# Half of the rows of a late w_down tile: their last 768 columns in eleven small transfers into the ring

## The chip, the cores and the metric

One core of a Trainium2 chip runs the kernel. The metric is the device time of one execution in microseconds (us), as a median of several runs. The core has five engines, here named as in the profile: PE (matrix multiply; PEld is its loading of weights), DVE (vector), ACT (scalar), POOL (GpSimd) and SP (sync), which here issues nearly all DMA transfers. The transfers run on 16 DMA engines.

## What is computed

One step of a decoder layer for a single token, with two branches on the same normalised input, both added to `x`. All is float32.

```
xn = layernorm(x)                                  # 1024
q  = xn @ wq                                       # 32 heads of 128
o  = softmax(q k^T / sqrt(128)) v                  # 4 kv heads, last 4096 cache rows
A  = o @ wo                                        # 4096 x 1024
h  = gelu(xn @ w_gate) * (xn @ w_up)               # 3584
B  = h @ w_down                                    # 3584 x 1024
out = x + A + B
```

With one token, each weight is read once and used once.

## The kernel before

**Staging.** All weights and the two caches pass through one SBUF tile, `ring`, of 128 partitions by 32,768 floats. `PLAN` (L256 to L263) lists the loads in order: a key, its place in the ring, and the key whose use must be done before it. `used(key)` (L346) issues the loads that wait for `key`. The semaphores are worked out by `Flow` (L54): it records each instruction, finds which earlier ones it overlaps in memory, and on a second pass gives each DMA a semaphore of its own and each reader the waits it needs. All instructions go through L99 to L107, so the profile shows one line for nearly everything, L225.

**The end of the run.** `wo` comes as `o0` and `o1` (16 tiles each, a tile being 128 rows by 1024 columns). `w_down` has 28 tiles: `d0` has 16, `d1` 8, `d2` 4. `d1` and `d2` go where `o1` was, so they are issued as the tiles of `o1` are used up. `d2` is at column 24,576 of the ring; each partition holds 4 rows of `w_down`, one for each tile, 4,096 bytes apiece.

`outputs` (L724) and `downs` (L734) multiply. A tile is used in one of two ways. `accumulate` (L715) makes four PE matmuls into the PSUM tile `out_p`, one for each quarter of the columns. `add_scaled` (L417) makes one DVE instruction that adds the tile, scaled by a number per partition, into the SBUF tile `out_part`. In `downs`, DVE takes the six tiles in `KEPT`, all of `d0`; PE takes the rest, folds in `out_part`, and then takes the tiles of `d2`.

The last tile is treated apart (L749 to L768). After tile 2 of `d2` DVE makes `y = out_p + x_out`. PE multiplies columns 0 to 511 of the last tile into `first_p`, DVE adds it to the first half of `y`, and two stores are issued. PE multiplies columns 512 to 1023 into `last_p`, and DVE adds it in two pieces to `y_last`, each followed by a store.

**How `d2` is loaded (L319 to L330).** Tiles 0 and 1 of `d2` are taken as 2,048 columns of 128 partitions. Partitions 0, 2, 4... come whole in one transfer (64 x 2048), partitions 1, 5, 9... whole in one (32 x 2048). Partitions 3, 7, 11... come without their last 768 columns (32 x 1280); these columns of the ring are zeroed by a POOL memset (L321), so that the matmuls on them add nothing. Tile 2 comes in one transfer, and tile 3 in three: columns 0 to 511, 512 to 767 and 768 to 1023 (L328, where `end == rows` picks the last tile; `rows` is the number of tiles, 4).

The 32 x 768 values left out have a buffer of their own, `moved` (L332), loaded by ten small transfers of 3 or 5 rows (`load_moved`, L335), which `PLAN` puts between `o1` and `d0`. `hidden` (L664) gathers the matching values of `h` with four small matmuls and four DVE copies into `moved_h`, and `downs` adds the product with two `add_scaled` (L737, L738).

Of the kernel before, what the change touches and what calls it, by code (L numbers as in the profile page):

```python
# [5 lines left out]
F32 = mybir.dt.float32  # L6
# [5 lines left out]
P = 128  # L12
D = 1024
# [19 lines left out]

ROW = (31, 32, 95, 96)
MC = 768
MOVED = ((0, 0, 0, 12, 4), (0, 1, 12, 12, 4), (1, 0, 24, 5, 1), (1, 1, 29, 3, 1))
SIZES = {"tp": NB, "acc": 2 * NB, "part": 8 * NB, "rows": 2 * NB}


# [14 lines left out]
class Flow:  # L54
# [4 lines left out]
    def __init__(self, nc, plan=None):  # L59
        self.nc = nc  # L60
        self.plan = plan
        self.ops = []
        self.touched = {}
        self.sems = {}
        if self.plan:
            inc = self.plan[-1][1]
            self.last = inc
            used = {key for waits, _ in self.plan for key, _ in waits}
            used.update(inc for _, inc in self.plan if inc is not None)
            for key in [*sorted(used - {inc}), ISSUED, inc]:  # L70
                self.sem(key)
        self.first = None
        for name in ("tensor", "vector", "scalar", "gpsimd", "sync"):
            setattr(self, name, Queue(self, getattr(nc, name)))
# [62 lines left out]
        self.ops.append((engine, dma, needs))  # L137

    def planned(self, stores):

        known = {}
        after = []
        waits = []
        counted = set()
        for k, (engine, dma, needs) in enumerate(self.ops):
            mine = known.setdefault(engine, {})
            asked = []
            latest = {}
            for d in needs:
                key = ("d", d) if self.ops[d][1] else ("e", self.ops[d][0])  # L150
                latest[key] = max(latest.get(key, -1), d)
            for key, d in sorted(latest.items(), key=lambda x: -x[1]):
                if mine.get(key, -1) >= d:
                    continue
                asked.append((key, d))
                for other, tick in after[d].items():
                    mine[other] = max(mine.get(other, -1), tick)
                mine[key] = max(mine.get(key, -1), d)
            asked = [
                (key, d) for n, (key, d) in enumerate(asked)  # L160
                if not any(after[later].get(key, -1) >= d for _, later in asked[:n])
            ]
            waits.append(asked[::-1])
            counted.update(d for _, d in asked)
            done = dict(mine)
            done[("d", k) if dma else ("e", engine)] = k
            after.append(done)
        ticks, totals = {}, {}
        for k in sorted(counted):
            engine, dma, _ = self.ops[k]  # L170
            if not dma:
                totals[engine] = totals.get(engine, 0) + 1
                ticks[k] = totals[engine]
        plan = []
        for k, (engine, dma, _) in enumerate(self.ops):
            inc = None
            if dma:
                inc = ("d", stores[-1] if k in stores else k)
            elif k in ticks:
                inc = ("e", str(engine).split(".")[-1])  # L180
            plan.append((
                [
                    (("d", d), 16) if key[0] == "d"
                    else (("e", str(key[1]).split(".")[-1]), ticks[d])
                    for key, d in waits[k]
                ],
                inc,
            ))
        return plan
# [38 lines left out]
class Pool:  # L228
# [34 lines left out]
]  # L263

# [1 line left out]
def decode_layer(nc, x, k_cache, v_cache, wq, wo, w_gate, w_up, w_down, out):  # L266
# [32 lines left out]

    def load(key, at):  # L300
        kind, i = key
        if kind == "m":
            load_moved()
            return
        src = source(*key)
        if kind in "kv":

            loaded[key] = dst = ring[:, at:at + RING // 4]
            if kind == "v":
                nc.sync.dma_start(dst, src)  # L310
            else:
                for odd in range(2):
                    nc.sync.dma_start(dst[odd:P:2], src[:, odd])
            return
        rows, n = src.shape[1:]
        loaded[key] = ring[:, at:at + rows * n]
        dst = loaded[key].rearrange("p (t n) -> p t n", n=n)
        pieces = PIECES[i] if kind == "d" else (0, rows)
        if key == ("d", 2):  # L319
            end = 2 * n - MC  # L320
            nc.gpsimd.memset(loaded[key][:, end:2 * n], 0.0)  # L321
            both = src[:, 0:2].rearrange("p t n -> p (t n)")
            nc.sync.dma_start(loaded[key][0:P:2, :2 * n], both[0:P:2])
            nc.sync.dma_start(loaded[key][1:P:4, :2 * n], both[1:P:4])
            nc.sync.dma_start(loaded[key][3:P:4, :end], both[3:P:4, :end])
            pieces = pieces[1:]
        for t, end in zip(pieces, pieces[1:]):
            ends = (0, n // 2, 3 * n // 4, n) if key == ("d", 2) and end == rows else (0, n)  # L328
            for cols in (slice(*cut) for cut in zip(ends, ends[1:])):
                nc.sync.dma_start(dst[:, t:end, cols], src[:, t:end, cols])  # L330

    moved = consts.tile([P, 2, MC], F32, name="moved")  # L332
    moved_h = consts.tile([P, 2], F32, name="moved_h")

    def load_moved():  # L335


        rest = w_down[DF - 4 * P:, D - MC:].rearrange("(r x) n -> x r n", x=16)[13]
        for s, a, first, count, step in MOVED:
            for j in range(step):  # L340
                to = 32 * a + j
                nc.sync.dma_start(
                    moved[to:to + 4 * (count // step):4, s], rest[first + j:first + count:step]
                )

    def used(key):  # L346

# [30 lines left out]

    hz = consts.tile([P, TD + 1, 32], F32, name="hz")
    nc.vector.memset(hz, 0.0)  # L380
    nc.gpsimd.memset(moved, 0.0)
    nc.gpsimd.memset(moved_h, 0.0)
    oz = consts.tile([P, HQ + 1, 32], F32, name="oz")
    nc.vector.memset(oz, 0.0)
    units = consts.tile([P, 2, 32], F32, name="units")
# [62 lines left out]
    def add_scaled(total, w, factor, first):  # L448

        if first:  # L450
            nc.vector.tensor_scalar(total, w, factor, None, op0=ALU.mult)
        else:
            nc.vector.scalar_tensor_tensor(total, w, factor, total, op0=ALU.mult, op1=ALU.add)
# [210 lines left out]
    def hidden():  # L664

        h_p = small("h_p")
        kept = ((0, 16, 0, 4), (1, 8, 0, 2), (1, 4, 2, 1))
        t = at = 0  # L670
        for b, count, c, n in kept:
            k = rows[b]
            m = NB // count
            flat = copies[b][:k].rearrange("p a n -> p (a n)")
            for i in range(count):
                nc.tensor.matmul(
                    h_p[:, at + i:at + n * count:count], flat[:, i:P * count:count],
                    ident[:k, 32 * c:32 * (c + n):32], start=True, stop=True,
                )
            for own in range(n):  # L680
                r = slice(m * own, m * own + m)
                cols = slice(at + count * own, at + count * own + count)
                nc.vector.tensor_copy(hz[r, t:t + count, 31], h_p[r, cols])
            t, at = t + count, at + n * count
        k = rows[1]
        flat = copies[1][:k, 0]
        spans = []
        for s, a, first, count, step in MOVED:
            start = 16 * first + 13
            taken = flat[:, start:min(start + 80 * step, NB):4 * step]  # L690
            n = taken.shape[1]
            nc.tensor.matmul(
                h_p[32 * a:32 * a + n, at + s:at + s + 1], taken, ident[:k, 64:65],
                start=True, stop=True,
            )
            spans.append((slice(32 * a, 32 * a + n), s))
        for r, s in spans:
            nc.vector.tensor_copy(moved_h[r, s:s + 1], h_p[r, at + s:at + s + 1])


    out_p = psum.tile([P, CO], F32, name="out_p", tag="out")
# [32 lines left out]
    def downs():  # L734

        tiles = [loaded["d", i][:, n * D:(n + 1) * D] for i in range(3) for n in range(DOWN[i])]
        for s in range(2):  # L737
            add_scaled(out_part[:52, D - MC:], moved[:52, s], moved_h[:52, s:s + 1], False)  # L738
        for t in KEPT:
            add_scaled(out_part, tiles[t], hz[:, t, 31:32], False)  # L740
        order = [t for t in range(DOWN[0]) if t not in KEPT]
# [31 lines left out]
    half = RING // 8  # L773
    for key, _, _ in PLAN:
        kind, i = key
        if kind == "m":
            continue
        if kind == "q":
            project("q", i, loaded.pop(key), range(NR), 8)
        elif kind == "k":  # L780
# [70 lines left out]
```

## Time and profile before

| | |
|---|---|
| time, median of 3 runs | 226.18 us (226.03 to 226.19) |
| span of the profiled execution, first to last instruction | 224.8 us |
| moved by DMA | 94.53 MB, mean 421 GB/s |
| PE busy | 126.0 us (56%) |
| DVE busy | 112.1 us (50%) |
| ACT busy | 28.2 us (13%) |
| POOL busy | 2.8 us (1%) |
| mean granted PE clock | 0.795 of full speed |

The span leaves out what lies before the first and behind the last instruction; the time of a run is 1.4 us above it. Busy time counts an engine's own work and no waits. A row of the timeline gives start, length, engine, operation, what it writes and reads, count, and in brackets the idle time before it with what ended it. A row of the chain gives start, length and what held the end of the run at that time. A row of the windows gives the stretch, its length, the busy time of PE, PEld, DVE, ACT and POOL with the instructions in it, the granted clock, the mean busy share of the 16 DMA engines (a small overlap can put it over 1), and GB/s.

### The profile page before, as it was taken

Reading aid. Unit: us, or ns where it says so; the run is one execution under the profiler, and the core shown is the slowest. Engines: PE = TensorE matmul, PEld = TensorE weight load, DVE = VectorE, ACT = ScalarE, POOL = GpSimd, SP = SyncE. Lnnn points to the kernel's source line nnn. Section 1 sums busy time; section 2 is a strip of 40 time slices with the busy share of each in tenths; the row PEclk is TensorE's granted clock in tenths of the full one; section 3 lists DMA queues with packets and bytes.
Section 4 is the critical chain, followed back from the end, with each engine's and each line's share of the span. In section 5 each row is a group of like instructions: output and inputs, shape, how many; then the busy total and the mean of one; then the engine's idle time right before and its main releaser. Section 6 shows DMA issues by size and latency. Waiting matters only on the chain.

```text
span 224.8 us, 2511 instructions
## 1 busy us (share of the span) xinstructions
PE 126.0 (56%) x1107; PEld 65.6 (29%) x1107; DVE 112.1 (50%) x142; ACT 28.2 (13%) x54; POOL 2.8 (1%) x9
## 2 busy tenths in 40 slices
PE   0120910539899891999836751237308988900976
PEld 0010200104634731755601110001003887400442
DVE  7030920591333282336039489339708932992942
ACT  2030000002415600454400220000000000000000
POOL 3000000000000000000000000000000000010000
PEclk9999975596969999799988795557965855665699
DMA  9889889799997999999989999999989989999994
GB/s 374 374 385 548 373 373 560 338 408 464 439 490 338 429 443 452 391 488 408 472 355 449 434 449 429 490 399 420 469 385 455 467 385 461 434 397 394 426 407 172
DMA packets 3194, 94.53 MB, mean 421 GB/s; under 512 B 446, under 2 KB 718, under 8 KB 1040
## 3 DMA queue, kind: packets, MB, share of 16 engines
q1 hardware_dynamic: 3160, 94.38, 97.8%
q8 instruction: 8, 0.13, 0.2%
q14 instruction: 2, 0.02, 0.0%
q10 hardware_dynamic: 24, 0.01, 0.0%
HBM read 94.38 MB, written 0.00 MB: 420 GB/s over the span
## 4 chain that ended last, share of the span: by engine, by line
DMA 67%; DVE 20%; PE 10%; SPq 1%; ACT 1%; issue 1%; POOL 0%; DVEq 0%
DMA ring<-in_B_w_gate 26%; DMA ring<-in_A_wq 18%; DMA ring<-in_A_wo 13%; DVE part L225 13%; DMA ring<-in_B_w_down 10%; PE tp L225 6%; PE out L225 3%; DVE out_part L225 3%; DVE rows L225 2%; SPq L225 1%; PE acc L225 1%; DVE g_sb L225 1%; ACT kT L225 1%; DVE hz L225 1%; DVE kT L225 0%
## 5 line engine op out<-in xcount | busy, mean ns | idle before, releaser
L225 PE MATMUL acc<-ring,xz 128*32 128x512 f32 x176 | 32.2, 808 | 37.3 <-DMA ring<-in_A_wq 22.2
L225 DVE SCALAR_TENSOR_TENSOR part<-ring,xz,part 128x3584 f32<-128x3584 f32 (+1 forms) x9 | 37.2, 4129 | 22.0 <-DMA ring<-in_A_wq 12.5
L225 PE MATMUL tp<-ident,ring 128*128 128x128 f32 x128 | 21.0, 309 | 7.1 <-DMA ring<-in_A_k_cache 5.0
L225 PEld LDWEIGHTS acc<-ring,xz 128*32 128x32 f32 x176 | 7.2, 139 | 58.2 <-issue 26.7
L225 DVE SCALAR_TENSOR_TENSOR out_part<-ring,oz,out_part 128x1024 f32<-128x1024 f32 x16 | 20.6, 1285 | 0.6
L225 PEld LDWEIGHTS tp<-ident,ring 128*128 128x128 f32 x128 | 15.4, 154 | 16.7 <-DMA ring<-in_A_k_cache 5.9
L225 PE MATMUL out<-ring,hz 128*32 128x256 f32 x168 | 12.1, 438 | 13.5 <-DMA ring<-in_B_w_down 13.4
L225 DVE COPY kT<-tp 128x512 f32<-128x512 f32 x12 | 8.1, 690 | 19.1 <-PE tp L225 19.1
L225 PE MATMUL out<-ring,oz 128*32 128x256 f32 x120 | 12.0, 586 | 9.6 <-DMA ring<-in_A_wo 9.6
L225 ACT ACTIVATE kT<-tp 128x512 f32<-128x512 f32 x20 | 11.5, 596 | 26.6 <-PE tp L225 26.6
L225 PE MATMUL tp<-ident,kT 128*128 128x4 f32 (+4 forms) x64 | 13.4, 343 | 1.6 <-DVE hz L225 1.6
L225 PEld LDWEIGHTS tp<-ident,kT 128*128 128x128 f32 (+2 forms) x64 | 13.1, 294 | 2.2 <-DVE hz L225 1.8
L225 PE MATMUL acc<-part,units 128*32 128x512 f32 x44 | 8.1, 817 | 8.7 <-DVE part L225 8.7
L225 DVE TENSOR_SCALAR part<-ring,xz 128x3584 f32<-128x3584 f32 (+1 forms) x3 | 6.5, 2171 | 12.3 <-DMA ring<-in_A_wq 7.5
L225 PEld LDWEIGHTS out<-ring,hz 128*32 128x32 f32 x168 | 5.6, 125 | 20.0 <-DMA ring<-in_B_w_down 15.8
L225 PEld LDWEIGHTS out<-ring,oz 128*32 128x32 f32 x120 | 5.7, 166 | 16.0 <-DMA ring<-in_A_wo 10.6
L225 DVE SCALAR_TENSOR_TENSOR out_part<-ring,hz,out_part 128x1024 f32<-128x1024 f32 x6 | 7.7, 1285 | 4.9 <-DMA ring<-in_B_w_down 4.7
L225 PE MATMUL s<-kT,qz 128*32 128x512 f32 x64 | 9.3, 709 | 0.0
L225 DVE TENSOR_REDUCE m<-s 128x2 f32<-128x1024 f32 x4 | 4.9, 1225 | 7.7 <-PE s L225 7.7
L225 PE MATMUL o<-ring,pT 128*32 128x128 f32 x256 | 7.8, 274 | 1.0 <-ACT pT L225 1.0
L225 PEld LDWEIGHTS o<-ring,pT 128*32 128x32 f32 x256 | 6.7, 110 | 1.9 <-ACT pT L225 1.9
L225 PE MATMUL tp<-ident,x_rows 2*128 2x2 f32 x4 | 0.6, 253 | 10.4 <-DMA x_rows<-in_A_x 10.4
(96 smaller groups left out, 73.3 us busy)
## 6 DMA issues: line engine op xcount, KB each, us to landing
ring<-in_B_w_gate SPq DMA_DIRECT2D x2, 7168.0 KB, 29.5
ring<-in_A_k_cache SPq DMA_DIRECT2D x4, 2048.0 KB, 19.0
ring<-in_A_v_cache SPq DMA_DIRECT2D x2, 4096.0 KB, 26.1
ring<-in_B_w_up SPq DMA_DIRECT2D x2, 3584.0 KB, 22.3
ring<-in_B_w_up SPq DMA_DIRECT2D x1, 7168.0 KB, 25.8
ring<-in_B_w_down SPq DMA_DIRECT2D x2, 2048.0 KB, 20.7
ring<-in_B_w_down SPq DMA_DIRECT2D x2, 512.0 KB, 21.1
ring<-in_B_w_down SPq DMA_DIRECT2D x2, 256.0 KB, 21.2
```

The source lines that it names most:

```text
L225: return lambda *a, **k: self.flow.issue(self.engine, lambda: call(*a, **k))
```

## The change

`moved`, `moved_h`, their loads, memsets, matmuls, copies and adds go, and the memset in the ring too. In tiles 0 and 1 of `d2`, all odd partitions (64) now come in two parts, both straight into the ring: their last 768 columns in eleven transfers of 9, 9, 9, 9, 9, 3, 3, 3, 3, 3 and 4 partitions, and their first 1,280 columns in one transfer of 64 partitions. The eleven share one semaphore: `Flow.shared` lists them, and a reader waits for 16 x 11 on it.

```diff
-MOVED = ((0, 0, 0, 12, 4), (0, 1, 12, 12, 4), (1, 0, 24, 5, 1), (1, 1, 29, 3, 1))
+SPREAD = (9, 9, 9, 9, 9, 3, 3, 3, 3, 3, 4)
...
+        groups = {k: group for group in (stores, self.shared) for k in group}
...
-            for d in needs:
+            for d in {groups[n][-1] if n in groups else n for n in needs}:
...
-                inc = ("d", stores[-1] if k in stores else k)
+                inc = ("d", groups[k][-1] if k in groups else k)
...
-                    (("d", d), 16) if key[0] == "d"
+                    (("d", d), 16 * len(groups.get(d, (d,)))) if key[0] == "d"
...
-    (("o", 0), 0, ("ub", 0)), (("o", 1), 16384, ("u", 1)), (("m", 0), None, ("u", 1)),
+    (("o", 0), 0, ("ub", 0)), (("o", 1), 16384, ("u", 1)),
...
         if key == ("d", 2):
-            end = 2 * n - MC
-            nc.gpsimd.memset(loaded[key][:, end:2 * n], 0.0)
             both = src[:, 0:2].rearrange("p t n -> p (t n)")
-            nc.sync.dma_start(loaded[key][0:P:2, :2 * n], both[0:P:2])
-            nc.sync.dma_start(loaded[key][1:P:4, :2 * n], both[1:P:4])
-            nc.sync.dma_start(loaded[key][3:P:4, :end], both[3:P:4, :end])
+            whole, cut = loaded[key][0:P:2, :2 * n], loaded[key][1:P:2, :2 * n]
+            nc.sync.dma_start(whole, both[0:P:2])
+            at = 0
+            for count in SPREAD:
+                nc.shared.append(len(nc.ops))
+                rows = slice(1 + 2 * at, 2 * (at + count), 2)
+                nc.sync.dma_start(loaded[key][rows, 2 * n - MC:2 * n], both[rows, 2 * n - MC:])
+                at += count
+            assert at == P // 2
+            nc.sync.dma_start(cut[:, :2 * n - MC], both[1:P:2, :2 * n - MC])
             pieces = pieces[1:]
         for t, end in zip(pieces, pieces[1:]):
             ends = (0, n // 2, 3 * n // 4, n) if key == ("d", 2) and end == rows else (0, n)
...
-    moved = consts.tile([P, 2, MC], F32, name="moved")
-    moved_h = consts.tile([P, 2], F32, name="moved_h")
...
-                nc.sync.dma_start(
-                    moved[to:to + 4 * (count // step):4, s], rest[first + j:first + count:step]
-                )
...
-    nc.gpsimd.memset(moved, 0.0)
-    nc.gpsimd.memset(moved_h, 0.0)
...
-            nc.tensor.matmul(
-                h_p[32 * a:32 * a + n, at + s:at + s + 1], taken, ident[:k, 64:65],
-                start=True, stop=True,
-            )
...
-            nc.vector.tensor_copy(moved_h[r, s:s + 1], h_p[r, at + s:at + s + 1])
...
-        for s in range(2):
-            add_scaled(out_part[:52, D - MC:], moved[:52, s], moved_h[:52, s:s + 1], False)
```

The loop over `SPREAD` uses the name `rows` for a slice of partitions. That name held the number of tiles, 4, which the unchanged last lines compare with `end`.

SP's queue from the loads of `wo` up to the last load, before (`in_B_w_down` is `w_down`; sizes are partitions by floats):

```order
L225 DMA ring<-in_A_wo 128x16384 x2
L225 DMA moved<-in_B_w_down 3x768 x8
L225 DMA moved<-in_B_w_down 5x768
L225 DMA moved<-in_B_w_down 3x768
L225 DMA ring<-in_B_w_down 128x16384
L225 DMA ring<-in_B_w_down 128x4096 x2
L225 DMA ring<-in_B_w_down 64x2048
L225 DMA ring<-in_B_w_down 32x2048
L225 DMA ring<-in_B_w_down 32x1280
L225 DMA ring<-in_B_w_down 128x1024
L225 DMA ring<-in_B_w_down 128x512
L225 DMA ring<-in_B_w_down 128x256 x2
```

The same place after the change:

```order
L226 DMA ring<-in_A_wo 128x16384 x2
L226 DMA ring<-in_B_w_down 128x16384
L226 DMA ring<-in_B_w_down 128x4096 x2
L226 DMA ring<-in_B_w_down 64x2048
L226 DMA ring<-in_B_w_down 9x768 x5
L226 DMA ring<-in_B_w_down 3x768 x5
L226 DMA ring<-in_B_w_down 4x768
L226 DMA ring<-in_B_w_down 64x1280
L226 DMA ring<-in_B_w_down 128x1024 x2
```

The small transfers have moved from ahead of `d0` into the middle of `d2`, and the last tile, which came as 128x512 and 128x256 twice, now comes as 128x1024, like tile 2.

DVE from the copies of `h` to the sum after the last tiles but one, before (`hz` holds `h`, `tp` is PSUM):

```order
L225 COPY hz<-tp 128x4
L225 COPY moved_h<-tp 20x1 x3
L225 COPY moved_h<-tp 9x1
L225 SCALAR_TENSOR_TENSOR out_part<-ring,oz,out_part 128x1024 x8
L225 SCALAR_TENSOR_TENSOR out_part<-moved,moved_h,out_part 52x768 x2
L225 SCALAR_TENSOR_TENSOR out_part<-ring,hz,out_part 128x1024 x6
L225 TENSOR_TENSOR y<-out,x_out 128x256
```

The same place after the change:

```order
L226 COPY hz<-tp 64x8 x2
L226 COPY hz<-tp 128x4
L226 SCALAR_TENSOR_TENSOR out_part<-ring,oz,out_part 128x1024 x8
L226 SCALAR_TENSOR_TENSOR out_part<-ring,hz,out_part 128x1024 x6
L226 TENSOR_TENSOR y<-out,x_out 128x256
```

DVE no longer makes the four copies ahead of the tiles of `o1` and the two adds ahead of those of `d0`.

More of the change, by code (lines that the diff above doesn't have):

```diff
@@ L62, in __init__ @@
         self.ops = []
+        self.shared = []
         self.touched = {}
@@ L301, in load @@
         kind, i = key
-        if kind == "m":
-            load_moved()
-            return
         src = source(*key)
@@ L330, in load @@
                 nc.sync.dma_start(dst[:, t:end, cols], src[:, t:end, cols])
-    moved = consts.tile([P, 2, MC], F32, name="moved")
-    moved_h = consts.tile([P, 2], F32, name="moved_h")
[L335 to L341, printed above, removed]
-                nc.sync.dma_start(
-                    moved[to:to + 4 * (count // step):4, s], rest[first + j:first + count:step]
-                )
     def used(key):
@@ L684, in hidden @@
             t, at = t + count, at + n * count
[L685 to L691, printed above, removed]
-            nc.tensor.matmul(
-                h_p[32 * a:32 * a + n, at + s:at + s + 1], taken, ident[:k, 64:65],
-                start=True, stop=True,
-            )
-            spans.append((slice(32 * a, 32 * a + n), s))
-        for r, s in spans:
-            nc.vector.tensor_copy(moved_h[r, s:s + 1], h_p[r, at + s:at + s + 1])
     out_p = psum.tile([P, CO], F32, name="out_p", tag="out")
@@ L775, in decode_layer @@
         kind, i = key
-        if kind == "m":
-            continue
         if kind == "q":
```

## Prediction

> **What bounds the kernel now.** I read the page first, then the chain of waits, the windows over the end of the run, and the timeline of its last seven microseconds. The page's chain and its DMA part:
>
> ```profile
> span 224.8 us, 2511 instructions
> DMA 67%; DVE 20%; PE 10%; SPq 1%; ACT 1%; issue 1%; POOL 0%; DVEq 0%
> q1 hardware_dynamic: 3160, 94.38, 97.8%
> q8 instruction: 8, 0.13, 0.2%
> ```
>
> The kernel streams 94 MB; its queue q1 keeps the 16 DMA engines 97.8% busy over the whole span. So issue times, waits of the compute engines and idle POOL matter only where the stream runs dry, and the end is set by two things: when the slowest engine delivers the last bytes, and what must be computed behind them. The chain over the last part:
>
> ```profile
> 190.23 0.15 DVE moved_h L225
> ...
> 197.51 0.75 POOL ring L225
> 198.27 0.52 SPq L225
> ...
> 200.11 21.38 DMA ring<-in_B_w_down
> 221.49 0.04 issue
> 221.53 0.68 PE out L225 x8
> 222.22 0.02 issue
> 222.24 0.43 DVE y L225
> ...
> 222.77 0.29 DVE y L225
> 223.06 0.22 DVE y_last L225
> 223.28 0.03 issue
> 223.31 0.29 DVE y_last L225
> ```
>
> The chain goes through POOL's memset and SP, but the transfer issued at 200.11 lands 21.38 us later: it stands in a queue. That transfer is tile 2 of `d2` (the last but one of all 28). The last tile behind it does not appear as a wait on this chain: by the time DVE has made `y` from tile 2 (222.24 + 0.43), the first half of the last tile is already multiplied. The windows, columns as busy time of each engine, granted clock, DMA share, GB/s:
>
> ```profile
> 0.00:150.00 150.00, 79.71 (x693) 39.15 (x697) 66.81 (x99) 28.17 (x54) 2.06 (x8) 0.84 1.00 427
> 190.00:206.00 16.00, 6.21 (x72) 3.13 (x70) 12.89 (x14) 0.00 (x0) 0.74 (x1) 0.61 1.02 438
> ...
> 220.40:220.60 0.20, 0.20 (x8) 0.11 (x6) 0.00 (x0) 0.00 (x0) 0.00 (x0) 1.00 0.76 287
> 220.80:221.00 0.20, 0.20 (x12) 0.04 (x4) 0.00 (x0) 0.00 (x0) 0.00 (x0) 1.00 0.71 277
> 221.80:222.00 0.20, 0.20 (x8) 0.00 (x0) 0.00 (x0) 0.00 (x0) 0.00 (x0) 1.00 0.56 195
> 222.00:222.10 0.10, 0.10 (x4) 0.00 (x0) 0.00 (x0) 0.00 (x0) 0.00 (x0) 1.00 0.33 113
> 222.20:222.30 0.10, 0.10 (x4) 0.10 (x8) 0.06 (x1) 0.00 (x0) 0.00 (x0) 1.00 0.12 41
> 222.30:222.40 0.10, 0.10 (x8) 0.03 (x4) 0.10 (x1) 0.00 (x0) 0.00 (x0) 1.00 0.03 10
> ```
>
> The share is near three quarters from 220.4 on: about four engines have nothing left more than a microsecond before the others. The other twelve run out between 221.7 and 222.4. Why they differ is partly on the page: the eight `q8` packets took 0.2% of 16 engines' span, 0.002 x 16 x 224.8 / 8 = 0.9 us each, and whichever engine fetched one is late by that.
>
> **The change: what is off the path.** These go away:
>
> ```profile
> L225 POOL MEMSET ring<- 128x768 f32 x1 | 0.7, 737 | 194.9 <-DVE out_part L225 194.9
> L225 DVE SCALAR_TENSOR_TENSOR out_part<-moved,moved_h,out_part 52x768 f32<-52x768 f32 x2 | 2.0, 1010 | 0.1
> L225 SPq DMA_DIRECT2D moved<-in_B_w_down x10: 641/642/798, 158.3 to 164.7; - x10
> L225 SPq DMA_DIRECT2D ring<-in_B_w_down x10: 327/432/590, 180.8 to 201.7; - x10
> 208.24 7.89 DVE L225 SCALAR_TENSOR_TENSOR out_part<-ring,hz,out_part 128x1024 f32<-128x1024 f32 x6 [4.73 <-DMA ring<-in_B_w_down]
> ```
>
> DVE loses two adds of 1.01 us and four copies of 0.15 us, PE four small matmuls, POOL 0.74 us. I cost all of it at nothing: DVE has 4.73 us of idle time before 208.24, when `d0` lands, and would only wait longer. Were that cover gone it would be 2.0 + 0.6 + 0.74 = 3.3 us. SP's first issue for `d2` comes earlier by the memset (0.75) and the copies (0.6), at about 197. Its issues then take 0.5 for the whole rows, eleven small ones at 0.64 (the `moved` row) = 7.1, and three at about 0.5: finished near 206. Nothing but the output stores stands behind them on SP. The stream does not run dry (share 1.02 over 190 to 206), and a transfer issued at 200.11 needed 21.38 us, so the issue has some ten microseconds to spare. Zero.
>
> **The bytes of each DMA engine.** A busy engine moves 427 / 16 = 26.7 GB/s (first window), so a 3,072 byte row takes 0.115 us, 5,120 bytes 0.19, 8,192 bytes 0.31. The views name no engine. I take a transfer of 9, 5, 4 or 3 rows to lie on the first 9, 5, 4 or 3 engines, one row each; the other bound is an even deal, which changes nothing. Then an engine has, over `moved` and the first two tiles of `d2`:
>
> - before: 6 x 8,192 + 2 x 5,120 each; the first three 10 rows of 3,072 more, the next two one row more;
> - after: 4 x 8,192 + 4 x 5,120 each; the first three 11 rows more, the fourth 6, the fifth to ninth 5, the last seven none.
>
> The differences are -3,072 bytes (-0.12 us) for the first three, +9,216 (+0.35) for the fourth, +6,144 (+0.23) for the fifth, +9,216 (+0.35) for four more, -6,144 (-0.23) for the last seven. Six engines get more, and only about four are early in the windows above, so at least two of the six are among the late twelve. The twelve are spread over 0.7 us. With two of them put 0.35 later, the last end moves somewhere from -0.2 (none of the six near the end) to +0.35 (one of them is the last). I take +0.1.
>
> [...]
>
> **The last tile.** The order shows something that the few words on the change do not say. In the new loop `rows` is bound to a slice, so the later test `end == rows` is never true for `d2`, and the last tile's three transfers (columns 0 to 511, 512 to 767, 768 to 1023) become one. The timeline of PE and DVE at the end:
>
> ```profile
> 217.98 1.93 PE L225 MATMUL out<-ring,hz 128*32 128x256 f32 x32 [1.25 <-DMA ring<-in_B_w_down]
> 220.25 1.07 PE L225 MATMUL out<-ring,hz 128*32 128x256 f32 x16
> 221.53 0.64 PE L225 MATMUL out<-ring,hz 128*32 128x256 f32 x8 [0.21 <-DMA ring<-in_B_w_down]
> 222.18 0.43 PE L225 MATMUL tp<-ring,hz 128*32 128x128 f32 x8
> 222.54 0.69 PE L225 MATMUL acc<-ring,hz 128*32 128x128 f32 x8
> 223.00 0.60 DVE L225 TENSOR_TENSOR y_last<-y,acc 64x128 f32<-64x128 f32 x2
> ```
>
> Before, `first_p` (the `tp` group) starts at 222.18 on the first half, beside the transfer of the rest; DVE adds it to `y` at 222.77 and ends at 223.31 + 0.29 = 223.60. After, `first_p` must wait for the whole tile. Tile 2, 512 KB in one transfer, made PE wait from the start at 220.25 to 221.53: 1.28 us apart. The last tile, the same size, then lands 1.28 after 221.49, at 222.77. Behind it, by these rows: PE starts 0.04 later, 0.43 for `first_p` (223.24), 0.03 to DVE, 0.29 for `y` (223.56), 0.22 and 0.03 and 0.29 for the two `y_last` adds: 224.10. That is +0.50 against 223.60. The matmuls of `acc` run beside DVE's add and are not the last wait. At the full 26.7 GB/s the tile's 32 KB per engine need 1.23 us, which gives +0.45. The old pieces have rows of 2 and 1 KB, and while they run the engines move less: 277 / (0.71 x 16) = 24.4 and 113 / (0.33 x 16) = 21.4 GB/s; so at best one transfer of full rows saves 16 KB / 24.4 + 16 KB / 21.4 - 1.23 = 0.2 us: lower bound +0.3. I take +0.45.
>
> **Sum.** 0 + 0.1 + 0.45 = +0.55 us on a span of 224.8. The measured median, 226.18, is 1.4 above that span; I leave this part as it is. 226.18 + 0.55 = 226.7. Since a small transfer can hardly be free of cost (next part), I put the forecast at 226.8. A measurement of this kernel can tell some 0.2%, or 0.45 us, from no change.
>
> **Rivals.**
>
> *Each small transfer costs its overhead.* The trace of before hides the ten `moved` transfers in a long queue, followed by 8 MB in which an engine could catch up. After, only the rest of `d2` stands behind the eleven, and an engine has little time to catch up in. If a row takes twice its 0.115 us, five rows cost 0.58 more and eleven 1.27 more; the first three engines were relieved by 0.12 and are not known to be last, so I price it at +0.6 to +1.2 on the last end, +1.15 to +1.65 in all: about 227.5. For it: 1 KB rows at the end run at 21.4 GB/s instead of 26.7. Against it: 20% is not 100%, and the rows are 3 KB. [...] Chance 0.12.
>
> *The gain and the loss cancel.* The last engines are all among the seven relieved by 0.23, and the single last transfer saves its 0.2: -0.23 + 0.3 = +0.07, 226.25; with either alone 226.4 to 226.5. For it: twelve late engines, of which the seven may well be most. Against it: at least two of the six with more bytes are late. PE limits the gain too: it waits only 0.21 us for tile 2 (row 221.53), so tile 2 landing earlier than that brings nothing. Chance 0.29. This is "same".
>
> *Faster.* It needs more than 0.45 us. The whole imbalance is about four engines idle for 1.5 us, 6 / 16 = 0.38 us if it were dealt out perfectly, and the last tile's chain stands against it. It could only be if the last tile were still cut in three, or if the removed work were on the path after all, against the 4.73 us of idle time. Chance 0.04.
>
> **How the numbers follow.** Forecast as summed, +0.45 to +0.95: chance 0.55. With the overhead rival, 0.12, slower by over 0.2% has 0.67. Same 0.29, faster 0.04. The range goes from 226.3 (+0.1, leaving out faster and the lowest part of the cancelling case) to 227.3 (leaving out the upper half of the overhead rival).
>
> **What would show it.** Right: `first_p` starting after 222.7, DVE's three last adds back to back behind it, ending some 1.3 us after the last landing instead of within a microsecond; one 512 KB issue more and none of 256 and 128 KB; DVE's idle time before its `d0` adds up by some 3 us with no effect on the end; fewer engines early in the last windows, and the last bytes at 222.4 to 222.8. Wrong: if PE's wait for the last tile ends before 222.4, the balance gained more than I allow; if it ends after 223.2, the small transfers cost more; if `d0` is read earlier than 208.2, work I costed at nothing was on the path.

## The result, and the profile after

The changed kernel takes 227.66 us (median of 5 runs, 227.42 to 227.91) where the kernel before takes 226.13: a ratio of 1.0066, 95% interval 1.0055 to 1.0077. It is 1.53 us slower. "Slower" was forecast, but by 0.6 us; the time lies above the range of 226.3 to 227.3. The profiled execution after is the longest of the five (its span is 226.6 us), so the times below are up to 0.3 us longer than in a median run. In the kernel before, `add_scaled` stands at L448, not at L417 as said above.

The stream on the page of the changed kernel:

```profile
span 226.6 us, 2478 instructions
q1 hardware_dynamic: 2920, 94.38, 97.3%
```

The bytes are the same and the 16 engines count as busy as before (97.3%, 97.8% before). The time has not gone into idle DMA engines. The timeline of PE and DVE from the use of `d0` to the end, in the changed kernel:

```profile
208.34 7.89 DVE L226 SCALAR_TENSOR_TENSOR out_part<-ring,hz,out_part 128x1024 f32<-128x1024 f32 x6 [8.48 <-DMA ring<-in_B_w_down]
...
218.60 1.93 PE L226 MATMUL out<-ring,hz 128*32 128x256 f32 x32 [1.76 <-DMA ring<-in_B_w_down]
...
221.55 1.07 PE L226 MATMUL out<-ring,hz 128*32 128x256 f32 x16 [0.59 <-DMA ring<-in_B_w_down]
...
222.80 0.64 PE L226 MATMUL out<-ring,hz 128*32 128x256 f32 x8 [0.18 <-DMA ring<-in_B_w_down]
...
224.04 0.43 PE L226 MATMUL tp<-ring,hz 128*32 128x128 f32 x8 [0.60 <-DMA ring<-in_B_w_down]
...
224.53 0.29 DVE L226 TENSOR_TENSOR y<-y,tp 128x128 f32<-128x128 f32 x1 [0.60 <-PE tp L226]
224.74 0.59 DVE L226 TENSOR_TENSOR y_last<-y,acc 64x128 f32<-64x128 f32 x2
```

Set against the rows shown of before: `d0` is read at 208.34 (208.24 before), the second half of `d1` at 218.60 (217.98), tiles 0 and 1 of `d2` at 221.55 (220.25), tile 2 at 222.80 (221.53). So 1.3 us are lost between 217 and 222, on DMA waits, and no more up to tile 2. `d1` is late too, though its transfers are issued ahead of the small ones. Then `first_p` starts at 224.04 instead of 222.18, and DVE ends 1.73 us later: another 0.46 us in the last tile. Two losses, then, and both begin with the transfers of `d2`.

Where the first is lost shows in the windows. Before:

```profile
217.00:218.00 1.00, 0.02 (x3) 0.02 (x3) 0.00 (x0) 0.00 (x0) 0.00 (x0) 1.00 0.94 381
218.00:219.00 1.00, 1.00 (x20) 0.66 (x24) 0.00 (x0) 0.00 (x0) 0.00 (x0) 1.00 0.95 392
219.00:220.00 1.00, 1.00 (x28) 0.52 (x17) 0.00 (x0) 0.00 (x0) 0.00 (x0) 1.00 0.99 394
```

and after the change:

```profile
217.00:218.00 1.00, 0.00 (x0) 0.00 (x0) 0.00 (x0) 0.00 (x0) 0.00 (x0) 1.00 0.97 284
218.00:219.00 1.00, 0.40 (x8) 0.29 (x12) 0.00 (x0) 0.00 (x0) 0.00 (x0) 1.00 0.99 286
219.00:220.00 1.00, 1.00 (x28) 0.60 (x20) 0.00 (x0) 0.00 (x0) 0.00 (x0) 1.00 0.98 313
```

The last two columns are the DMA share and GB/s. In this stretch, in which the small transfers run, the engines are as busy (0.97 to 0.99, against 0.94 to 0.99) and move 284 + 286 + 313 = 883 KB in 3 us instead of 1,167. The share is the mean over the 16 engines, so a late or idle one would lower it; here the busy engines are slow.

### The profile page after: what moved, and what is told of

Read it like the earlier page. It is cut to its first block, busy times and chain, and to the rows that moved or that the text cites. A ratio compares the mean times of both kernels' runs of the same rounds, so it can differ in the third digit from the quotient of the medians.

```text
span 226.6 us, 2478 instructions
## 1 busy us (share of the span) xinstructions
PE 122.6 (54%) x1099; PEld 64.8 (29%) x1099; DVE 109.4 (48%) x136; ACT 28.0 (12%) x54; POOL 0.7 (0%) x6
## 3 DMA queue, kind: packets, MB, share of 16 engines
q1 hardware_dynamic: 2920, 94.38, 97.3%
## 4 chain that ended last, share of the span: by engine, by line
DMA 65%; DVE 19%; PE 9%; SPq 4%; ACT 1%; issue 1%; DVEq 0%
DMA ring<-in_B_w_gate 26%; DMA ring<-in_A_wq 18%; DMA ring<-in_A_wo 13%; DVE part L226 13%; DMA ring<-in_B_w_down 8%; PE tp L226 6%; SPq L226 4%; DVE out_part L226 3%; PE out L226 2%; DVE rows L226 2%; DVE g_sb L226 1%; ACT kT L226 1%; DVE hz L226 1%; PE acc L226 0%; DVE kT L226 0%
## 5 line engine op out<-in xcount | busy, mean ns | idle before, releaser
L226 PE MATMUL out<-ring,hz 128*32 128x256 f32 x168 | 11.6, 425 | 16.1 <-DMA ring<-in_B_w_down 16.1
L226 PE MATMUL out<-ring,oz 128*32 128x256 f32 x120 | 11.5, 566 | 9.5 <-DMA ring<-in_A_wo 9.5
L226 PE MATMUL tp<-ident,kT 128*128 128x4 f32 (+2 forms) x56 | 13.1, 366 | 1.3 <-DVE hz L226 1.3
L226 PEld LDWEIGHTS tp<-ident,kT 128*128 128x128 f32 (+1 forms) x56 | 12.8, 319 | 1.9 <-DVE hz L226 1.5
L226 PE MATMUL acc<-part,units 128*32 128x512 f32 x44 | 7.4, 757 | 8.2 <-DVE part L226 8.2
L226 PEld LDWEIGHTS out<-ring,oz 128*32 128x32 f32 x120 | 5.1, 160 | 15.8 <-DMA ring<-in_A_wo 10.4
L226 PE MATMUL s<-kT,qz 128*32 128x512 f32 x64 | 7.7, 598 | 0.0
```

The lines of the kernel that those rows point to most:

```text
L226: return lambda *a, **k: self.flow.issue(self.engine, lambda: call(*a, **k))
```

## The experiments

Two theories at the start: the last tile in one piece costs some 0.5 us; the eleven small transfers cost the rest, either because their rows go to neighbouring partitions, or as overhead of each transfer, or through uneven bytes of the engines. The experiments ran in three sets, each on a chip of its own and in turn with the kernel before, whose median was 226.13 beside the changed kernel, 226.16 in the first set (last tile, rows far apart, one transfer), 226.09 in the second (four transfers, own, same) and 226.20 in the third (shifted, and the last row). The third column takes each kernel from the kernel before of its own set, and kernels of different sets are compared by it.

| kernel | us | us over before | ratio to before, 95% interval |
|---|---|---|---|
| changed kernel | 227.66 | 1.53 | 1.0055 to 1.0077 |
| last tile in three pieces again | 227.31 | 1.15 | 1.0035 to 1.0068 |
| before, last tile in one piece | 226.68 | 0.52 | 1.0014 to 1.0032 |
| small transfers, rows far apart | 227.49 | 1.33 | 1.0041 to 1.0071 |
| one transfer in place of eleven | 226.85 | 0.69 | 1.0018 to 1.0041 |
| four transfers of 16 rows, near | 227.74 | 1.65 | 1.0058 to 1.0092 |
| four transfers of 16 rows, far | 227.39 | 1.30 | 1.0044 to 1.0074 |
| eleven, to own partitions of a spare buffer | 226.77 | 0.68 | 1.0020 to 1.0047 |
| eleven, to the same partitions of a spare buffer | 227.63 | 1.54 | 1.0054 to 1.0084 |
| eleven, shifted by 16 partitions in the spare buffer | 228.52 | 2.32 | 1.0086 to 1.0116 |
| one transfer, last tile in three pieces | 226.41 | 0.21 | 1.0001 to 1.0020 |

### The last tile

In the changed kernel, the slice gets a name of its own:

```diff
-                rows = slice(1 + 2 * at, 2 * (at + count), 2)
-                nc.sync.dma_start(loaded[key][rows, 2 * n - MC:2 * n], both[rows, 2 * n - MC:])
+                odd = slice(1 + 2 * at, 2 * (at + count), 2)
+                nc.sync.dma_start(loaded[key][odd, 2 * n - MC:2 * n], both[odd, 2 * n - MC:])
```

> The changed kernel with the slice renamed, so that the last tile comes in three transfers again; the eleven small transfers stay. Theory (two costs: the last tile in one piece is worth 0.5 us, the eleven transfers 1.0 to 1.2 us): 227.66 - 0.5 = 227.1 to 227.2, and DVE ends 0.8 to 0.9 us after the last landing as before the change, not 1.3. Rival (the last tile's cut is hidden, all of the loss is in the small transfers): 227.6 to 227.7.

Measured: 227.31, 0.35 us less than the changed kernel. The other way round, in the kernel before:

```diff
-            ends = (0, n // 2, 3 * n // 4, n) if key == ("d", 2) and end == rows else (0, n)
+            ends = (0, n)
```

> The kernel before with the last tile in one transfer, and nothing else changed. Theory (the one piece alone costs 0.5 us): 226.13 + 0.45 to 0.5 = 226.6. Rival (it is hidden, or the 2 and 1 KB rows that it saves make up for it): 226.0 to 226.2.

Measured: 226.68, 0.52 us over 226.16. The timeline of this kernel's end, with DVE and PE:

```profile
221.51 0.64 PE L225 MATMUL out<-ring,hz 128*32 128x256 f32 x8 [0.18 <-DMA ring<-in_B_w_down]
222.22 0.42 DVE L225 TENSOR_TENSOR y<-out,x_out 128x256 f32<-128x256 f32 x1 [6.08 <-PE out L225]
...
222.75 0.43 PE L225 MATMUL tp<-ring,hz 128*32 128x128 f32 x8 [0.60 <-DMA ring<-in_B_w_down]
...
223.24 0.29 DVE L225 TENSOR_TENSOR y<-y,tp 128x128 f32<-128x128 f32 x1 [0.60 <-PE tp L225]
223.45 0.60 DVE L225 TENSOR_TENSOR y_last<-y,acc 64x128 f32<-64x128 f32 x2
```

Tile 2 is read at 221.51, as in the kernel before (221.53), and DVE ends at 223.45 + 0.60 = 224.05 instead of 223.60. DVE now has 0.60 us of idle time ahead of its add to `y`: it waits for `first_p`, which waits for the whole tile. So the last tile's theory stands: 0.35 to 0.5 us, by itself.

### Rows far apart

Transfers of 9 and 3 rows again, and one of a single row, but the rows of a transfer 14 or 42 partitions apart (a list of first row, count, step):

```diff
-SPREAD = (9, 9, 9, 9, 9, 3, 3, 3, 3, 3, 4)
+SPREAD = (
+    (0, 9, 7), (1, 9, 7), (2, 9, 7), (3, 9, 7), (4, 9, 7),
+    (5, 3, 21), (12, 3, 21), (19, 3, 21), (6, 3, 21), (13, 3, 21), (20, 3, 21), (63, 1, 1),
+)
...
-            for count in SPREAD:
+            for at, count, step in SPREAD:
...
-                rows = slice(1 + 2 * at, 2 * (at + count), 2)
+                rows = slice(1 + 2 * at, 2 * (at + (count - 1) * step + 1), 2 * step)
```

> The changed kernel with the same rows in small transfers of 9 and 3 rows, but the rows of one transfer lie 14 or 42 partitions apart instead of 2 (one transfer of 1 row is left over, so twelve). Bytes for each engine are the same to within one row. Theory (neighbouring partitions: while a transfer's rows go to partitions close together, all engines slow down; 284 GB/s at a DMA share of 0.97 between 217 and 218 us, 381 before): the rate from 217 to 220 returns to 380 or more and the time to 226.6 to 226.9. Rival overhead (each small transfer costs, wherever it goes): 227.6 to 227.8. Rival bytes (the six engines with more bytes are the last): 227.6 to 227.7.

Measured: 227.49, the slow stretch as before (292, 299 and 285 GB/s from 217 to 220). My theory that neighbouring partitions are the cause fell.

### One transfer

With the loop of the experiment just shown:

```diff
-SPREAD = (9, 9, 9, 9, 9, 3, 3, 3, 3, 3, 4)
+SPREAD = ((0, 64, 1),)
```

> The changed kernel with the 64 rows of 768 columns in one transfer in place of eleven, dealt evenly to the engines; the last tile is in one piece. Theory (neighbouring partitions) and rival overhead both: the slow stretch goes, 226.13 + 0.5 for the last tile + 0.2 for the 6 KB more on the engines that end last = 226.8. Rival bytes: the same 226.8. If it stays at 227.4 or more, the eleven transfers are not the cause, but the split of all odd rows at 1280 columns.

Measured: 226.85. Its windows:

```profile
217.00:218.00 1.00, 0.11 (x4) 0.12 (x8) 0.00 (x0) 0.00 (x0) 0.00 (x0) 1.00 0.96 383
218.00:219.00 1.00, 1.00 (x22) 0.57 (x24) 0.00 (x0) 0.00 (x0) 0.00 (x0) 1.00 0.97 395
219.00:220.00 1.00, 1.00 (x24) 0.51 (x16) 0.00 (x0) 0.00 (x0) 0.00 (x0) 1.00 1.01 404
```

No slow stretch, with the same 3 KB rows. The eleven transfers cost 227.66 - 226.85 = 0.8 us.

### Four transfers of sixteen rows

Sixteen rows to a transfer are meant to give each engine one row, an even deal; no view names an engine. Near, a transfer fills 32 neighbouring partitions; far, its rows are 8 partitions apart (the loop is the same, the comments are added here):

```diff
-SPREAD = (9, 9, 9, 9, 9, 3, 3, 3, 3, 3, 4)
+SPREAD = ((0, 16, 1), (16, 16, 1), (32, 16, 1), (48, 16, 1))    # near
+SPREAD = ((0, 16, 4), (1, 16, 4), (2, 16, 4), (3, 16, 4))       # far
```

> The changed kernel with the 64 rows of 768 columns in four transfers of 16 rows, those of one transfer 2 partitions apart: each transfer fills 32 neighbouring partitions. Every engine should get one row of each (sixteen rows). The last tile is in one piece, as in all kernels of this set. Theory count (each small transfer costs, so four cost 4/11 of the 0.8 us between the eleven, 227.66, and the one, 226.85): 227.1 to 227.2. Theory partitions (engines write to partitions that another engine's stream needs at the same time; sixteen engines into 32 partitions is the strongest form): 227.3 or more, a rate under 330 GB/s between 217 and 219. Theory deal (only the uneven number of rows for each engine costs): 226.8 to 226.9.

> As the kernel with four transfers of 16 neighbouring rows, but the rows of one transfer 8 partitions apart, so that each transfer spreads over all 128 partitions; bytes and count of transfers are the same. Theory count: 227.1 to 227.2, like its neighbour. Theory partitions: 226.8 to 226.9, rate 380 or more. Theory deal: 226.8 to 226.9.

Measured: 227.74 near, with 283, 343 and 296 GB/s from 217 to 220, and 227.39 far. The rates of the far one:

```profile
217.00:218.00 1.00, 0.00 (x0) 0.00 (x0) 0.00 (x0) 0.00 (x0) 0.00 (x0) 1.00 1.00 316
218.00:219.00 1.00, 0.89 (x18) 0.55 (x21) 0.00 (x0) 0.00 (x0) 0.00 (x0) 1.00 0.93 324
219.00:220.00 1.00, 1.00 (x24) 0.64 (x20) 0.00 (x0) 0.00 (x0) 0.00 (x0) 1.00 1.09 312
```

Near costs 0.96 us and far 0.61 us over one transfer, against 0.84 us for the eleven; if the deal is even, as meant, an uneven one is not needed for the loss. The count is out as a measure: four near cost as much as eleven. My theory of partitions, as I had written it, did not fit the far one either. What was left of it was a guess: not how close the rows lie to each other, but which engine carries which partition's row.

### Own, same and shifted partitions

Three kernels write the rows of the eleven transfers to a spare buffer of 128 x 2 x 768 floats; the 64 x 768 values are left out of the sum. The buffer is zeroed by POOL at the start, and a DVE copy waits for it ahead of the sum. They differ only in where row k, counted from 0, goes (comments added here):

```diff
-                nc.sync.dma_start(loaded[key][rows, 2 * n - MC:2 * n], both[rows, 2 * n - MC:])
+                to = slice(first, first + 4 * count - 3, 4)                    # own, shifted
+                nc.sync.dma_start(spare[to, slot], both[rows, 2 * n - MC:])    # own, shifted
+                nc.sync.dma_start(spare[rows, 0], both[rows, 2 * n - MC:])     # same
```

`first` and `slot` come from a list with one pair for each transfer. In own, `first` is 0, 1, 2, 3 in slot 0 and 0, 1, 2, 3, 33, 34, 35 in slot 1; in shifted each is 16 higher. The partitions of own, and its name, are a guess of mine at the engine of each row, which no view shows.

> The changed kernel with the same eleven transfers of the same rows, but written to a spare buffer, row k of a transfer to one of the partitions 4k to 4k+3 (only row 9 and a few of the others 32 partitions on). The 64 x 768 values are not used: the sum leaves them out and takes what lay in the ring. A DVE copy of one column waits for the buffer ahead of the sum y. [...] Theory partitions: no slow stretch, 380 GB/s or more from 217 to 220, 226.7 to 226.9. Theory count or deal: 227.5 to 227.7 like the changed kernel.

> Control of the kernel with own partitions: the same spare buffer and the same DVE copy, the values left out of the sum in the same way, but row k of a transfer goes to the partition it has in the changed kernel. All theories: 227.5 to 227.7, with the slow stretch. If it is fast, the target in the ring mattered and not the partitions.

> [...] Theory own (a row slows the stream when it goes to partitions that another engine serves): the slow stretch is back, 227.4 to 227.7. Rival spacing (a step of 4 partitions is what makes it fast, the engine does not matter): 226.7 to 226.9.

Measured: own 226.77, same 227.63, shifted 228.52. The windows of own:

```profile
217.00:218.00 1.00, 0.06 (x4) 0.06 (x8) 0.00 (x0) 0.00 (x0) 0.00 (x0) 1.00 0.93 344
218.00:219.00 1.00, 1.00 (x20) 0.62 (x24) 0.00 (x0) 0.00 (x0) 0.00 (x0) 1.00 0.99 393
219.00:220.00 1.00, 1.00 (x27) 0.52 (x16) 0.00 (x0) 0.00 (x0) 0.00 (x0) 1.00 1.04 419
```

of same:

```profile
217.00:218.00 1.00, 0.00 (x0) 0.00 (x0) 0.00 (x0) 0.00 (x0) 0.00 (x0) 1.00 0.99 268
218.00:219.00 1.00, 0.74 (x16) 0.48 (x20) 0.00 (x0) 0.00 (x0) 0.00 (x0) 1.00 1.03 281
219.00:220.00 1.00, 1.00 (x24) 0.58 (x20) 0.00 (x0) 0.00 (x0) 0.00 (x0) 1.00 0.95 301
```

and of shifted:

```profile
217.00:218.00 1.00, 0.00 (x0) 0.00 (x0) 0.00 (x0) 0.00 (x0) 0.00 (x0) 1.00 1.02 257
218.00:219.00 1.00, 0.49 (x12) 0.32 (x16) 0.00 (x0) 0.00 (x0) 0.00 (x0) 1.00 1.02 210
219.00:220.00 1.00, 1.00 (x24) 0.62 (x20) 0.00 (x0) 0.00 (x0) 0.00 (x0) 1.00 0.94 209
```

Same lies 1.54 us over the kernel before and the changed kernel 1.53, so the spare buffer, its memset and the copy cost nothing that can be seen. Count, sizes, source rows and spacing of own and shifted are the same; only the first partition differs, and 1.64 us lie between them (0.68 and 2.32 over the kernel before). So eleven small transfers cost nothing that can be seen (0.68 us over the kernel before, against 0.69 for one) when row k lands in partitions 4k to 4k+3 or 32 on, and 0.9 to 1.6 us in these kernels when it lands elsewhere. Own has the eleven transfers and the rows of the changed kernel, so their sizes and number alone cost nothing that can be seen either. The windows agree in this: at a share of 0.93 to 1.04, the rate is 209 to 301 GB/s in same and shifted, and 344 to 419 in own. The runs show this dependence on the partition; what the busy engines wait for, no view shows.

The traces also keep the time of each DMA packet, and show which rows pay. Averages over the rows of tiles 0 and 1 of `d2`:

| ns for a row of | one transfer | own | changed kernel | shifted |
|---|---|---|---|---|
| 3,072 bytes (small transfers) | 122 | 127 | 153 | 192 |
| 5,120 bytes (64 x 1280) | 199 | 202 | 264 | 350 |
| 8,192 bytes (64 x 2048) | 320 | 322 | 370 | 438 |

The 64 rows of 5,120 bytes are loaded alike in all four. In the changed kernel 61 of them took longer than the longest with one transfer, 206 ns: nearly the whole transfer is slow, and not only a few of its rows. In own, 2 of them did, and 5 of the 64 small rows took longer than the longest small row with one transfer, 128 ns (46 in the changed kernel). Summed over all rows of `d2`, the changed kernel spends 12.4 us more than the kernel with one transfer, or 0.78 us for each of 16 engines on average, where the medians differ by 0.81; shifted spends 27.7 us more than own, or 1.73 us for each engine, where the times over the kernel before differ by 1.64. Of the 12.4 us only 2.0 are in the small rows themselves. The rest falls on rows of the large transfers around them.

### Both costs taken out

One transfer of 64 rows, and the last tile in three pieces:

```diff
-SPREAD = (9, 9, 9, 9, 9, 3, 3, 3, 3, 3, 4)
+SPREAD = (64,)
...
-                rows = slice(1 + 2 * at, 2 * (at + count), 2)
-                nc.sync.dma_start(loaded[key][rows, 2 * n - MC:2 * n], both[rows, 2 * n - MC:])
+                odd = slice(1 + 2 * at, 2 * (at + count), 2)
+                nc.sync.dma_start(loaded[key][odd, 2 * n - MC:2 * n], both[odd, 2 * n - MC:])
```

> The changed kernel with both costs taken out: the 64 rows of 768 columns in one transfer and the last tile in three. [...] Theory (the three costs add: 0.5 for the last tile, 0.8 for the small transfers, the rest of 1.5 for the lost balance): 226.85 - 0.45 = 226.4. Rival (the buffer brought nothing): 226.1 to 226.2.

Measured: 226.41 against 226.20 (1.0001 to 1.0020). What is left, some 0.2 us, is near the edge of what the runs can tell. It may be the balance that the buffer was meant to give, but this kernel also cuts twice as many odd rows in two, and no run separates the two. In steps from the changed kernel back to the one before, 227.66 - 226.85 = 0.81 us go with the eleven transfers, 226.85 - 226.41 = 0.44 with the last tile and 0.21 with the rest. That such steps add up to the whole (1.46 of 1.53 us) is no test of them. A test is that the last tile is worth 0.52, 0.44 and 0.35 us in three different kernels: about the same, and a little less beside the eleven transfers. No kernel here beats the one before.

## Why the prediction was wrong

- *Work off the path, costed at nothing: right.* DVE's idle time ahead of `d0` grew from 4.73 to 8.48 us and `d0` was still read at 208.3. The chain of waits of the changed kernel now leads through SP's small issues; its end shows why that is no loss:

```profile
205.19 0.58 SPq L226
205.77 0.04 issue
205.81 18.18 DMA ring<-in_B_w_down
224.00 0.04 issue
224.04 0.47 PE tp L226 x8
```

  The last issue ends near 206, as worked out, and its data lands 18.18 us later: it still stands in a queue.
- *The last tile, +0.45 (bounds 0.3 and 0.5): right.* 0.52 when added to the kernel before, 0.44 with one transfer, 0.35 with the eleven. One reading behind it was loose: the 1.28 us lie between two starts on PE, and at the first, 220.25, PE had not waited for data, so they are not the distance of two landings. The changed kernel, where both starts wait, gives 224.04 - 222.80 = 1.24 us, close to the 1.23 that the prediction had from the rate.
- *The bytes of each engine, +0.1 (bounds -0.2 and +0.35): this step failed.* It priced a row by its bytes at the rate of a busy engine, 0.115 us, wherever the row goes, and said of an even deal that it changes nothing. Four transfers of sixteen rows, meant as an even deal, cost 0.61 us (far) and 0.96 us (near) over one transfer; own, with the same transfers as the changed kernel, costs nothing over it (0.68 us over the kernel before, against 0.69). What counted were the partitions that the small rows go to: in the changed kernel the rows of the other transfers slowed down too (5,120 bytes: 264 ns, against 202 in own and 199 with one transfer). The deal that it took, as many engines as a transfer has rows, fits the packet counts: q1 has 3,160 packets before and 2,920 after. The rows of `moved` and `d2` are 672 before and 448 after; that the other packets are 16 fewer is right if a transfer adds one packet for each engine that it runs on: 32 + 7 x 16 = 144 against 64 + 4 x 16 = 128. That the rows lie on the first engines, and with it the +0.1, no run shows; what the runs showed in its place is +0.8 for the transfers as they are, +1.0 with the 0.2 that is left over. The prediction's own sign for this came: PE's wait for the last tile ended at 224.04, after the 223.2 that it named for small transfers that cost more.
- *The rival of overhead, 227.5, chance 0.12: near in size, wrong in kind.* No run shows the small row at twice its 0.115 us that it was summed from. Eleven transfers of 9 to 27 KB at the same place in the queue (own) lie 0.68 us over the kernel before, against 0.69 for one, and their rows took 127 ns, against 122: behind the queued work here their overhead does not show. The step from 226.7 to 226.8, for a cost of small transfers as such, no run shows either.
- *Range and chances.* Slower had 0.67 and came, but of the 1.53 us only the last tile's 0.35 to 0.5 came in the way that was forecast. The range ended at 227.3, which is 1.1 us over 226.18 and just under the +1.15 at which the overhead rival begins: it left out the whole of that rival, and not its upper half as it says. (That rival's upper sum, +1.65, also lacks the 0.1 for the bytes that its lower sum holds.) A bound for a cost that no row of before shows should have reached the end of this rival.

Open: why shifted loses twice what same does. All its rows go to partitions 16 to 63, those of same to partitions 1 to 127, which may be it; no run separates that. What it is about the partitions that slows the stream, no run shows either. And which engine carries which row, and which engines end last, no view shows.

## What to carry to other kernels

Before rows are given to less loaded DMA engines, look at the partitions that they go to, and not only at the bytes of each engine. Here small transfers cost nothing that can be seen in own's partitions (0.68 us over the kernel before, against 0.69 for one transfer), and 0.6 to 1.6 us more in others; rows sent straight to their place in a tile keep that place's partitions. Read GB/s beside the DMA share: a full share at a low rate (0.97 to 0.99 at 284 to 313 in the changed kernel) was slow rows here (264 ns for 5,120 bytes instead of 199), and a falling share (0.76 at 287 GB/s at 220.4 us, 0.03 at 10 at 222.3, in the kernel before) was the end of the stream. And when code for one transfer is rewritten, look at the order of the issues behind it: a reused name turned three transfers into one and cost 0.35 to 0.5 us, a quarter to a third of the loss.

## What the hardware showed that I had not expected

Eleven small transfers behind a queue cost no more than one (0.68 against 0.69 us over the kernel before), but 192 KB of rows sent to other partitions than own's slow the whole stream from some 390 to as little as 209 GB/s for 3 to 4 us, with the engines shown as busy. In the changed kernel five sixths of the time lost is in rows of the large transfers around them, not in the small rows. Moving the target by 16 partitions, with nothing else changed, made 1.64 us.
